# Four of eight experts' places shrink from 124 to 120 and one grows from 148 to 150 in an attention, mixture-of-experts and feed-forward kernel

## The chip, the core and the metric

The kernel runs on one core of a Trainium2 chip. The metric is device time in microseconds (us): the median of timed executions of the whole program. The profile beside it is of one execution of its own. TensorE is called PE below; its weight loads have a row of their own, PEld. VectorE is DVE, ScalarE is ACT, GpSimd is POOL, SyncE is SP. SP and ACT also issue transfers, which the core's 16 DMA engines carry out.

## What is computed

The reference has three stages over 2304 tokens. The middle one, which the change touches, sends each token that passes a skip test to one of eight experts:

```python
def _moe_ref(x, w_skip, w_gate, w1, w2):
    do_compute = (x @ w_skip) > 0
    xc = x[do_compute]
    logits = xc @ w_gate
    e_idx = np.argmax(logits, axis=1)
    gate_w = softmax(logits)[arange, e_idx]
    for e in range(8):
        mask = e_idx == e
        h = np.maximum(xc[mask] @ w1[e], 0.0)
        y[mask] = gate_w[mask, None] * (h @ w2[e])
    out[do_compute] = xc + y
```

Ahead of it stands masked attention (4 batches, 8 heads, 576 positions, 64 wide), whose output is `x`; behind it a feed-forward layer (512 to 2048 to 512) with a piecewise quadratic activation. For the reference's inputs the eight experts get 166, 153, 145, 136, 113, 111, 106 and 87 tokens, in order of size.

## The kernel before

**Stages.** Attention and the routing come first. At their end POOL scatters each token, as a row of 515 float32 (512 values, a gate weight, a token's number in two parts), to a scratch tensor `scr` in HBM, where each expert has a region of its own. Then the experts run one after the other, and after them the feed-forward layer, which fills the rest of the program.

**Places.** The experts are ranked by their number of tokens. An expert of rank r gets `RANKED[r]` columns in every tile of its stage, whatever its true number; `ORDER` has them run by rank as 0, 4, 1, 5, 2, 6, 3, 7, so `CAP` is 168, 124, 156, 124, 148, 124, 140, 124. An expert with more tokens than places would go on in a loop behind the stage (`tc.If(ovf > 1)`), in chunks of `CF` columns. `CF` is the smallest entry of `RANKED`; it also sets `NCHUNK`, the length of the tables that this loop would read.

**An expert's rows.** `load_x(e)` loads the expert's rows from `scr` in two halves of `CAP[e] // 2` rows each, as tiles `xr` with one row in each partition (L759). For expert 0 SP and ACT issue one half each, for all others SP issues both. `prep_x` turns a half into columns on PE: one transpose for the gate weight (L774), four for the values (L776), one for the number (L777).

**An expert's matmuls.** Eight steps f. `emit_h` multiplies a weight tile by the expert's columns (L818, four matmuls, each of which the trace records twice), ACT applies the rectifier (L820), and `emit_y`, two steps later, multiplies by a tile of the second weight (L838, again four). A weight tile `wr` is 128 by 1024 float32, 524,288 bytes; an expert has eight, of which `emit_h` uses the even ones, each for two steps, and `emit_y` the odd ones. So steps 0 and 1 need tile 0, steps 2 and 3 tile 2, and step 4 tile 4. The next expert's halves are turned behind steps 3 and 4.

**Order of the loads.** SP's queue is in program order: the halves of expert 0, four weight tiles, the halves of expert 1, four more weight tiles, a tile `sk` of skipped tokens, four more weight tiles, and so on. Tiles of weights share slots with the raw weights of the last layer, which DVE, ACT and POOL decode during the experts (`decode`). PE runs a few empty matmuls (`stay_warm`, L176) where it would else be idle.

Of the kernel before, what the change touches and what calls it, by code (L numbers as in the profile page):

```python
# [40 lines left out]
LK, SK = QT + STR, 5 * NJ  # L41


RANKED = (168, 156, 148, 140, 124, 124, 124, 124)
C, CF = RANKED[0], RANKED[-1]
ORDER = (0, 4, 1, 5, 2, 6, 3, 7)
CAP = [RANKED[r] for r in ORDER]
W = DM + 3
# [1078 lines left out]
```

## Time and profile before

| | before |
|---|---|
| median of 3 timed runs | 692.84 us (691.78 to 695.59) |
| the profiled execution's own time | 686.14 us |
| its span, first to last instruction | 684.5 us |
| PE busy | 657.0 us, 96% of the span |
| granted TensorE clock, mean | 0.994 |

The span is what the trace covers; the profiled execution's own time holds 1.64 us more around it. The timed runs are other executions: their median is 6.70 us above the profiled one.

### The profile page before, as it was taken

The numbers are of one execution on the slowest core, as the hardware profiler recorded it, in microseconds if no ns is written. First come the engines' busy times: TensorE is split into PE (matmuls) and PEld (weight loads), VectorE is DVE, ScalarE is ACT, GpSimd is POOL, SyncE is SP. The second block draws the span as 40 slices with busy tenths as digits, with TensorE's granted clock in tenths as the row PEclk, the third lists the DMA queues.
The fourth block names the chain that finished last, engine by engine and source line by source line (L and its number), as shares of the span: only waits on it lengthen the run. The fifth ranks groups of instructions, "written<-read, shape, count | busy, mean of one in ns | idle before, by whom it ended". The sixth has DMA issues, their size and how long they took to land.

```text
span 684.5 us, 13286 instructions
## 1 busy us (share of the span) xinstructions
PE 657.0 (96%) x4766; PEld 588.4 (86%) x4768; DVE 391.4 (57%) x1223; ACT 289.1 (42%) x783; POOL 110.0 (16%) x175
## 2 busy tenths in 40 slices
PE   8999997799999998999999999999999999999996
PEld 5787784699999988889998998999899989998994
DVE  6988976347676765777643354335544543454332
ACT  5776650233333332555533343334433433353332
POOL 6553644022222221000010001000100010001001
PEclk9999999899999999999999999999999999999999
DMA  9898993999789964021010001000100010001001
GB/s 267 237 283 252 331 351 142 340 332 312 242 276 300 335 234 166 32 88 36 1 47 0 1 1 46 1 1 0 47 1 0 1 47 0 1 1 46 1 1 46
DMA packets 24337, 82.95 MB, mean 121 GB/s; under 512 B 3446, under 2 KB 3446, under 8 KB 24266
## 3 DMA queue, kind: packets, MB, share of 16 engines
q1 hardware_dynamic: 19640, 68.28, 31.0%
q0 software_dynamic: 2880, 9.47, 3.7%
q10 hardware_dynamic: 1746, 4.30, 1.8%
q8 instruction: 39, 0.64, 0.4%
q14 instruction: 32, 0.26, 0.1%
HBM read 72.57 MB, written 9.46 MB: 120 GB/s over the span
## 4 chain that ended last, share of the span: by engine, by line
issue 46%; PE 10%; POOL 2%; DVE 0%; POOLq 0%; ACT 0%; ACTq 0%; DVEq 0%
PE hp L1009 6%; PE po L1046 5%; POOL out_dram L180 2%; POOLq L1123 0%; DVE x L1055 0%; ACT r L1019 0%; DVE r L1023 0%; DVE r L1024 0%; DVE gl L1032 0%; ACT gh L1028 0%; ACT xh L989 0%; POOLq L180 0%; PE hp L1013 0%; ACTq L989 0%; DVEq L1024 0%
## 5 line engine op out<-in xcount | busy, mean ns | idle before, releaser
L1009 PE MATMUL hp<-xh,wd 128*128 128x384 f32 x768 | 196.4, 337 | 2.4 <-ACT xh L989 2.4
L1046 PE MATMUL po<-wd,gh 128*128 128x512 f32 x576 | 180.5, 395 | 0.0
L1009 PEld LDWEIGHTS hp<-xh,wd 128*128 128x128 f32 x768 | 140.2, 188 | 10.8 <-ACT xh L989 2.6
L1023 DVE SCALAR_TENSOR_TENSOR r<-r 128x384 f32<-128x384 f32 x96 | 53.6, 558 | 134.8 <-ACT r L1019 134.7
L1009 PE MATMUL hp<-xl,wd 128*128 128x384 f32 x384 | 129.3, 337 | 0.0
L1046 PEld LDWEIGHTS po<-wd,gh 128*128 128x128 f32 x576 | 106.5, 188 | 17.1
L1046 PE MATMUL po<-wd,gl 128*128 128x512 f32 x288 | 113.4, 394 | 0.0
L1019 ACT ACTIVATE r<-hp,half 128x384 f32<-128x384 f32 x96 | 55.7, 580 | 136.4 <-PE hp L1009 122.9
L1028 ACT CAST gh<-r 128x384 fp32r<-128x384 f32 x96 | 49.3, 514 | 89.3 <-DVE r L1024 75.3
L1032 DVE TENSOR_TENSOR gl<-r,gh 128x384 fp32r<-128x384 f32 x96 | 53.6, 558 | 54.6 <-ACT gh L1028 54.4
L180 POOL DMA_INDIRECT out_dram<-x,outid x18 | 18.0, 998 | 396.4 <-DVE x L1055 336.2
L818 PE MATMUL hpt<-x,wr 128*128 128x124 f32 (+4 forms) x512 | 73.6, 287 | 3.8 <-DMA wr<-in_we_dram 3.8
L838 PE MATMUL yp<-h,wr 128*128 128x124 f32 (+4 forms) x512 | 74.5, 290 | 1.9 <-issue 1.9
L1009 PEld LDWEIGHTS hp<-xl,wd 128*128 128x128 f32 x384 | 72.1, 188 | 0.4 <-DVE xl L990 0.4
L818 PEld LDWEIGHTS hpt<-x,wr 128*128 128x128 f32 x512 | 67.4, 193 | 4.5 <-issue 4.5
L838 PEld LDWEIGHTS yp<-h,wr 128*128 128x128 f32 x512 | 66.8, 193 | 3.9 <-issue 2.6
L1046 PEld LDWEIGHTS po<-wd,gl 128*128 128x128 f32 x288 | 54.1, 188 | 12.5
L421 ACT ACTIVATE pe<-sm,nm 128x90 f32<-128x90 f32 (+1 forms) x144 | 52.1, 364 | 26.5 <-DVE nm L414 22.0
L1024 DVE TENSOR_TENSOR r<-r,hp 128x384 f32<-128x384 f32 x96 | 53.2, 554 | 10.9 <-DVE r L1023 0.9
L1021 ACT ACTIVATE hp<-hp,half 128x384 f32<-128x384 f32 x96 | 52.3, 545 | 0.0
L723 POOL TENSOR_TENSOR wd<-da,wd 128x512 fp32r<-128x512 f32 x25 | 32.4, 1298 | 117.9 <-ACT wd L708 91.9
L708 ACT CAST wd<-da 128x512 fp32r<-128x512 f32 x32 | 19.8, 619 | 49.7 <-DVE da L711 43.2
(167 smaller groups left out, 696.1 us busy)
## 6 DMA issues: line engine op xcount, KB each, us to landing
wr<-in_we_dram SPq DMA_DIRECT2D x64, 512.0 KB
qk<-in_qk_dram SPq DMA_DIRECT2D x16, 592.0 KB
raw<-in_w_in_dram SPq DMA_DIRECT2D x16, 512.0 KB
v<-in_v_dram SPq DMA_DIRECT2D x15, 432.0 KB
raw<-in_w_out_dram SPq DMA_DIRECT2D x9, 512.0 KB
raw<-in_w_out_dram ACTq DMA_DIRECT2D x7, 512.0 KB
sk<-scr SPq DMA_DIRECT2D x12, 257.5 KB
xr<-scr SPq DMA_DIRECT2D x8, 124.7 KB
```

Of the source, the lines that this page charges most:

```text
L421: nc.scalar.activation(r["pe"][:, t, :N], r["sm"][:, t, :N], AF.Exp, bias=r["nm"][:, t:t + 1], scale=-1.0, accum_out=r["su"][:, t:t + 1])
L723: lambda: (V if late else nc.gpsimd).tensor_tensor(s["lo"], s["a"], s["hi"].bitcast(F32), op=ALU.subtract),
L818: nc.tensor.matmul(hpt, w[:, o:o + P], xg[e][:, c, :], start=c == 0, stop=c == 3)
L838: nc.tensor.matmul(yps[e][m // 2][:, m % 2], w[:, o:o + P], h, start=f == 0 and m % 2 == 0, stop=f == 7 and m % 2 == 1)
L1009: nc.tensor.matmul(hpt, w[:, c * P:(c + 1) * P], x, start=k == 0, stop=k == 11)
L1019: nc.scalar.activation(r, hpt, AF.Relu, bias=half[:, 0:1], scale=0.5)
L1021: nc.scalar.activation(u, hpt, AF.Relu, bias=half[:, 1:2], scale=0.5)
L1023: nc.vector.scalar_tensor_tensor(g, r, 1.0, r, ALU.min, ALU.mult)
L1024: nc.vector.tensor_tensor(g, g, u, op=ALU.add)
L1028: nc.scalar.copy(gh, g)
L1032: nc.vector.tensor_tensor(gl, g, gh.bitcast(F32), op=ALU.subtract)
L1046: nc.tensor.matmul(ops[bi][m], a[:, c], b_, start=f == 0 and k == 0, stop=f == NF - 1 and k == 2)
```

## The change

One line: `RANKED`, the table of places. In the order in which they run the experts get 168, 120, 156, 120, 150, 120, 140, 120 columns instead of 168, 124, 156, 124, 148, 124, 140, 124; the halves of rows are 84, 60, 78, 60, 75, 60, 70, 60 instead of 84, 62, 78, 62, 74, 62, 70, 62. `CF` becomes 120, and with it `NCHUNK` 20 instead of 19. A blank line ahead of the table moves every line number behind it up by one.

```diff
+
-RANKED = (168, 156, 148, 140, 124, 124, 124, 124)
+RANKED = (168, 156, 150, 140, 120, 120, 120, 120)
 C, CF = RANKED[0], RANKED[-1]
 ORDER = (0, 4, 1, 5, 2, 6, 3, 7)
 CAP = [RANKED[r] for r in ORDER]
```

No instruction moves past another; shapes change where they stand. SP's queue at the head of the experts' stage, before, from the last two of the first four weight tiles to the first two of the next four (`xr` are the halves of expert 1, `wr` the weight tiles, the loads from `tab` and `etab` fetch their addresses):

```order
L211 DMA wr<-in_we_dram 128x1024
L211 ISA
L211 DMA wr<-in_we_dram 128x1024
L197 TENSOR_LOAD etab
L759 ISA
L759 DMA xr<-scr 62x515
L756 TENSOR_LOAD tab
L759 ISA
L759 DMA xr<-scr 62x515
L211 ISA
L211 DMA wr<-in_we_dram 128x1024
```

The same place of the change:

```order
L212 DMA wr<-in_we_dram 128x1024
L212 ISA
L212 DMA wr<-in_we_dram 128x1024
L198 TENSOR_LOAD etab
L760 ISA
L760 DMA xr<-scr 60x515
L757 TENSOR_LOAD tab
L760 ISA
L760 DMA xr<-scr 60x515
L212 ISA
L212 DMA wr<-in_we_dram 128x1024
```

The two loads have 60 rows instead of 62, and stand where they stood. PE in expert 0, before, from step 3 of the first product (L818) to step 4, with the first half of expert 1 turned between them and the second product of step 1 (L838) behind it:

```order
L818 MATMUL hpt<-x,wr 128x168 x4
L774 MATMUL xtp<-idt,xr 128x62
L776 MATMUL xtp<-idt,xr 128x62 x4
L777 MATMUL xtp<-idt,xr 2x62
L838 MATMUL yp_2618<-h,wr 128x168 x2
L838 MATMUL yp_2619<-h,wr 128x168 x2
L818 MATMUL hpt<-x,wr 128x168 x4
```

The same place of the change:

```order
L819 MATMUL hpt<-x,wr 128x168 x4
L775 MATMUL xtp<-idt,xr 128x60
L777 MATMUL xtp<-idt,xr 128x60 x4
L778 MATMUL xtp<-idt,xr 2x60
L839 MATMUL yp_2618<-h,wr 128x168 x2
L839 MATMUL yp_2619<-h,wr 128x168 x2
L819 MATMUL hpt<-x,wr 128x168 x4
```

The transposes are two columns narrower; the matmuls of expert 0 and their order are the same.

## Rows read from the trace of the kernel before

**Rows 1.** The page: the span

```profile
span 684.5 us, 13286 instructions
```

**Rows 2.** By stretch: busy us of PE, PEld, DVE, ACT, POOL; clock, DMA share, GB/s

```profile
128.70:134.40 5.70, 2.05 (x15) 1.54 (x14) 1.89 (x5) 1.61 (x4) 1.26 (x1) 0.90 1.04 327
134.40:140.20 5.80, 5.71 (x23) 5.17 (x24) 0.94 (x3) 1.29 (x3) 0.21 (x1) 0.51 1.03 404
148.00:268.00 120.00, 118.06 (x1013) 115.58 (x1012) 82.73 (x176) 43.12 (x111) 28.63 (x22) 1.00 0.83 281
268.00:684.50 416.50, 407.37 (x2070) 367.09 (x2069) 202.72 (x382) 171.17 (x335) 17.96 (x18) 1.00 0.05 19
```

**Rows 3.** Timeline of PE, 122 to 143 us: start, us, what; idle before, its end

```profile
122.67 3.88 PE L818 MATMUL hpt<-x,wr 128*128 128x168 f32 x24 [0.96 <-DMA wr<-in_we_dram]
...
127.54 1.30 PE L818 MATMUL hpt<-x,wr 128*128 128x168 f32 x8
129.69 0.27 PE L774 MATMUL xtp<-idt,xr 62*128 62x62 f32 x1 [0.85 <-DMA xr<-scr]
...
130.20 1.41 PE L838 MATMUL yp<-h,wr 128*128 128x168 f32 x8
134.49 2.58 PE L818 MATMUL hpt<-x,wr 128*128 128x168 f32 x8 [2.88 <-DMA wr<-in_we_dram]
136.99 0.36 PE L774 MATMUL xtp<-idt,xr 62*128 62x62 f32 x1
...
137.82 2.53 PE L838 MATMUL yp<-h,wr 128*128 128x168 f32 x8
140.19 1.30 PE L818 MATMUL hpt<-x,wr 128*128 128x168 f32 x8
141.33 1.30 PE L838 MATMUL yp<-h,wr 128*128 128x168 f32 x8
```

**Rows 4.** Timeline of SP's queue: issues at the head of the experts' stage

```profile
120.71 1.52 SPq L759 DMA_DIRECT2D xr<-scr  x2
...
129.67 0.33 SPq L211 DMA_DIRECT2D wr<-in_we_dram  x1
...
133.28 0.33 SPq L211 DMA_DIRECT2D wr<-in_we_dram  x1
```

**Rows 5.** Waits of SP's queue, 119 to 137 us: us, times, longest

```profile
SPq L211 <- DMA xr<-scr: 5.9, 2, 3.1
```

**Rows 6.** By stretch, columns as in rows 2: behind 62-row halves, with 78-row halves

```profile
144.00:147.00 3.00, 3.00 (x23) 2.98 (x22) 1.57 (x4) 1.10 (x3) 0.55 (x1) 1.00 1.04 233
...
178.60:180.80 2.20, 2.20 (x20) 2.17 (x19) 0.64 (x2) 1.33 (x3) 1.17 (x1) 1.00 0.16 54
```

**Rows 7.** Waits of SP's queue, 194 to 211 us (62-row halves): us, times, longest

```profile
SPq L211 <- DMA xr<-scr: 2.9, 1, 2.9
SPq L792 <- DMA xr<-scr: 2.4, 1, 2.4
```

**Rows 8.** Waits of PE, 148 to 268 us, all of them

```profile
PE yp L838 <- issue: 1.9, 2, 1.3
```

**Rows 9.** Timeline of PE: neighbouring groups of 124, 148 and 140 columns

```profile
188.89 1.05 PE L838 MATMUL yp<-h,wr 128*128 128x124 f32 x8
189.78 1.06 PE L818 MATMUL hpt<-x,wr 128*128 128x124 f32 x8
...
211.91 1.17 PE L818 MATMUL hpt<-x,wr 128*128 128x148 f32 x8
212.91 1.17 PE L838 MATMUL yp<-h,wr 128*128 128x148 f32 x8
...
248.88 1.12 PE L838 MATMUL yp<-h,wr 128*128 128x140 f32 x8
249.83 1.12 PE L818 MATMUL hpt<-x,wr 128*128 128x140 f32 x8
```

**Rows 10.** By stretch, columns as in rows 2: most of an expert with 124 columns

```profile
187.50:204.00 16.50, 16.50 (x152) 16.45 (x152) 13.00 (x28) 6.12 (x15) 3.83 (x3) 1.00 0.82 271
```

## The prediction

> **What bounds the kernel now.** I read the profile from the whole to the one place where this change can matter. The profiled execution took 686.14 us, of which the trace spans 684.5 [rows 1]. Next the stretches: in the feed-forward stage PE is busy for 407.37 of 416.50 us with the DMA engines at a share of 0.05, and from 148 to 268 us, over seven of the eight experts, PE is busy for 118.06 of 120.00 [rows 2]. There the length is set by what PE executes, and no load can shorten it. The list of PE's waits in that stretch agrees: 1.9 us in two waits, both ahead of L838 and neither for a transfer [rows 8].
>
> The exception is the head of the experts' stage. From 128.70 to 134.40 us PE is busy for 2.05 of 5.70 us, and in the next 5.80 us it is busy at a granted clock of 0.51 [rows 2], the lower of its two levels, 1.2 instead of 2.4 GHz. The timeline says what it stands for. It waits 0.85 us for `xr`, the first half of expert 1 (62 rows), then 2.88 us for a weight tile [rows 3]. By the program that is tile 4 of expert 0, the first one that SP issues behind the two halves of 62 rows. After this pause the same groups of 168 columns that later start 1.14 us apart (140.19 to 141.33) take 2.4 to 2.5 us: 134.49 to 136.99 and 137.82 to 140.19 [rows 3].
>
> Why is tile 4 late? The halves were issued at 120.71 us, and SP's two issues of weight tiles at 129.67 and 133.28 were held for 5.9 us in sum by `xr` loads [rows 4, 5]. So each half was in flight for over 9 us. They are small: 62 x 515 x 4 = 127,720 bytes each, against 524,288 in a weight tile. At the 404 GB/s of the stretch from 134.40 [rows 2] both together are 0.63 us of all 16 engines. What is special is how few engines carry them. Behind a later pair of 62-row halves, when most of the queue has drained, the DMA share falls to 0.16 at 54 GB/s while weights are still on their way [rows 6]; one engine's part of 404 GB/s is 25.25, so this is what two engines move, and 2 of 16 are a share of 0.125. 62 is 2 times 31, and has no larger divisor up to 16. Two engines are therefore busy with 127,720 bytes each for both halves, 127,720 / 25.25 GB/s = 5.06 us, while the other fourteen go on. Every weight tile is spread over all 16, so each tile behind the halves is complete only when the two late engines are through.
>
> The sum confirms it. Tile 0 ends a wait of PE at 122.67 [rows 3]. Tiles 1 to 4 are 4 x 524,288 / 404 GB/s = 5.19 us, and the halves on two engines 5.06: tile 4 at 132.92. The stretch from 128.70 moved 327 GB/s instead of 404 at the same share [rows 2], which is 5.7 x (1 - 327/404) = 1.09 us more, 134.01; PE got it at 134.49.
>
> **Part 1, the halves of 62 and 74 rows become 60 and 75.** 60 and 75 are 4 and 5 times 15, so by the same reading of the row they lie on 15 engines. Then both halves cost 0.63 us instead of 5.06, and tile 4 lands at 122.67 + 5.19 + 0.63 = 128.5. The upper bound: in the stretch 144 to 147, where halves of 78 rows go through, all engines together moved 233 instead of 404 GB/s [rows 6], a loss of 3.0 x (1 - 233/404) = 1.27 us; with it tile 4 lands at 129.8. When does PE want it? Without the first wait the transposes start at 129.69 - 0.85 = 128.84; they take 0.51 (129.69 to 130.20), and the group of L838 behind them 1.14 [rows 3]. So step 4 is ready at 130.5, 0.7 to 2.0 us behind the tile. The first half itself comes at about 122.67 + 3 x 1.30 + 0.32 = 126.9, ahead of 128.84. Both waits go. With no pause PE has no reason to lose its clock: before 128.70 it was fed without a break of more than 0.96 us [rows 3].
>
> What that is worth: 0.85 + 2.88 = 3.73 us of waiting, and the lower clock. From 134.49 to 140.19 are 5.70 us; the same three groups at full clock are 1.14 + 0.10 + 0.51 + 1.14 = 2.89, where 0.10 is an allowance for the change from wide matmuls to transposes. That gives 2.81, together 6.54 us. What is late next? Nothing that I see: two tiles at the low rate of 233 GB/s take 4.5 us, and PE uses two tiles in two steps, four groups of 1.14 = 4.6 us. Between 148 and 268 us the 62- and 74-row halves also hold SP (2.9 and 2.4 us in one example [rows 7]), but no wait of PE there is for a transfer [rows 8], so I put the faster loads there at nothing; the cover is PE's own work, and if it were gone there would be more to gain, not less.
>
> The Trainium skill (DMA: Bandwidth & Descriptors, section "Why a DMA increments its semaphore by 16 and not by 1") says the same as a rule: such a load runs on the largest number of engines up to 16 that divides its outer dimension. By it 62 and 74 rows use 2 engines, 60 and 75 use 15. The trace shows the two, and no row of it shows a load of 60 or 75 rows; by the rule the sum is the one above.
>
> **Part 2, columns of the matmuls.** A group (four matmuls, eight records) starts 0.95 us after its neighbour at 140 columns, 1.00 at 148, and 0.89 at 124 [rows 9]. From 140 to 148 one column is 0.00625 us a group. Expert 4 has 16 groups, so two columns more cost 16 x 2 x 0.00625 = 0.20 us. On the same line 124 columns would be 0.85, but the row says 0.89: there the columns no longer decide. PEld is busy for 16.45 of 16.50 us in such an expert [rows 10], so loading the weights sets the pace, and a load of 128 columns is the same for 120 places. I take nothing for 124 to 120. The other end, if the line held, is 4 experts x 16 groups x 4 columns x 0.00625 = 1.60 us gained; 0.89 above the line speaks for the first.
>
> The skill (TensorE: Matmul & The Clock Gate, section "LDWEIGHTS") has a rule against a gain here as well: a weight load takes its columns divided by 1.2, in ns, so 107 for 128 columns however few are streamed. The row gives 0.89 / 8 = 111. By the rule the sum is unchanged.
>
> **Part 3, the rest.** DVE, ACT and the transposes handle 2 to 4 columns less in four experts and 1 or 2 more in one; the cover is PE, busy throughout [rows 2]. The tables grow from 152 to 160 numbers on DVE, while the first loads are on their way; if that cover were gone it would be a few per cent of five short instructions.
>
> **Sum.** 6.54 - 0.20 = 6.3 us: span 678.2, the profiled execution's own time 679.8. The timed median lies 6.70 us above that of the profiled execution; I let this stand and take 692.84 - 6.3 = 686.5 us. 0.5% is 3.5 us, about what a measurement of this kernel can tell from no change.
>
> **The rivals.**
>
> *Tile 4 is late all the same.* For it: packets also slow down where 78-row halves are read [rows 6], and now all 15 engines write rows at once. If all bytes from 122.67 on (four tiles and two halves of 60 rows, 2.34 MB) moved at 233 GB/s, tile 4 would land at 132.7, 2.2 us behind 130.5. Then PE waits again, and may lose its clock again: the gain is 1.3 us with the loss of 2.81, 4.1 without, so 688.7 to 691.5. Against it: the slow stretch was 3 us, not 10.
>
> *The change doesn't spread the loads, or the timed runs don't have the pause.* No row shows 60 rows, and the timed runs have no trace. Then only part 2 is left: 693.0 us.
>
> *Slower: the loop behind the experts runs.* An expert of rank 4 or later with 121 tokens would go through `tc.If(ovf > 1)`, and another pass over its weights is about one expert of 124 columns, 16.5 us [rows 10]: 686.5 + 16.5 = 703. It decides at the 121st token; the largest of these experts has 113. Even a DMA rate of 233 GB/s throughout is no way to slower: 132.7 is still ahead of 134.49.
>
> **How the numbers follow.** Forecast 0.70: own range 683.0 (with the 1.60 us of the columns, and both waits of [rows 8] gone) to 687.8 (tile 4 on the edge, with decoding, which loses its rest, costing PE another wait of 1.3 us like the longer one of [rows 8]). Late tile 0.12, no effect 0.12, slower 0.06 (half of it the loop, half what I don't see). The range runs from the forecast's lower end to the end of the late tile: 683.0 to 691.5, which leaves out 0.18. Faster by over 0.5%: the forecast and a third of the late tile, 0.74; within: 0.20; slower: 0.06.
>
> **What would show it.** In the profile of the changed kernel: no wait of PE for `wr` between 124 and 145 us, and none for `xr` of expert 1; granted clock 1.00 throughout these stretches; groups 1.14 us apart from step 3 of expert 0 on; SP's waits for `xr` at the head of the stage well below 5.9 us; no stretch with a DMA share of 0.16 while weights are due. Groups of 120 columns 0.89 us apart, those of 150 columns 1.01 to 1.02. I am wrong if the wait of 2.88 us is still there with loads that land early (then it wasn't the halves), if it moves to a later tile, or if the timed runs gain nothing where the profiled one does.

## The result and the profile after

The changed kernel takes 687.15 us in the median of 8 runs (685.74 to 689.21), the kernel before 692.93 us (691.3 to 695.59) beside it. The ratio is 0.9916, with a 95% interval of 0.9895 to 0.9937: 5.8 us faster, between 4.4 and 7.3. The forecast was 686.5 us, from 683.0 to 691.5. (A ratio here and below is the one on record for runs beside each other; it can differ a little from the quotient of the two medians.)

The spans of the two profiled executions say something else at first sight: 684.0 us after, 684.5 before [rows 1], where the forecast had 678.2 after. They differ in four places, so they have to be taken apart by stage. Start of the first transposes of the experts' stage and start of the last matmul of its second product, first before, then after (one line of the program each: its records, their shortest, median and longest time in ns, first and last start):

```profile
L774 PE MATMUL xtp<-idt,xr x16: 226/261/363, 120.1 to 246.4; 62*128 62x62 f32 x8, 84*128 84x84 f32 x2, 78*128 78x78 f32 x2, 74*128 74x74 f32 x2
L838 PE MATMUL yp<-h,wr x512: 269/282/647, 126.4 to 270.6; 128*128 128x124 f32 x85, 128*128 128x168 f32 x22, 128*128 128x140 f32 x22, 128*128 128x156 f32 x21
```

```profile
L775 PE MATMUL xtp<-idt,xr x16: 226/260/263, 125.5 to 244.0; 60*128 60x60 f32 x8, 84*128 84x84 f32 x2, 78*128 78x78 f32 x2, 75*128 75x75 f32 x2
L839 PE MATMUL yp<-h,wr x512: 264/282/410, 131.2 to 267.3; 128*128 128x120 f32 x85, 128*128 128x168 f32 x22, 128*128 128x140 f32 x22, 128*128 128x156 f32 x21
```

The experts' stage, from the first to the last of these, went from 150.5 to 141.8 us, 8.7 less. Attention, which no shape of the change touches, ended 5.4 us later in this one execution. The turn from the experts to the feed-forward stage was 1.4 us longer (the clock fell to half for 3.4 us there), and the feed-forward stage itself 1.5 us longer. Attention and the turn vary from execution to execution: over the twelve kernels below the first transposes start between 120.1 and 128.6 us, and the execution of before that was shown has the earliest of all. That is probably where most of the 6.70 us between its own time and the timed median lay; the timed runs have no trace to show it. Of the change the profiled execution took 685.74 us, only 1.41 less than the timed median.

The head of the experts' stage after, PE's timeline, to be laid beside [rows 3]:

```profile
127.56 3.78 PE L819 MATMUL hpt<-x,wr 128*128 128x168 f32 x24 [0.42 <-DVE x L779]
...
132.32 1.30 PE L819 MATMUL hpt<-x,wr 128*128 128x168 f32 x8
133.56 0.26 PE L775 MATMUL xtp<-idt,xr 60*128 60x60 f32 x1
...
134.05 1.41 PE L839 MATMUL yp<-h,wr 128*128 128x168 f32 x8
135.30 1.30 PE L819 MATMUL hpt<-x,wr 128*128 128x168 f32 x8
136.53 0.26 PE L775 MATMUL xtp<-idt,xr 60*128 60x60 f32 x1
...
137.03 1.41 PE L839 MATMUL yp<-h,wr 128*128 128x168 f32 x8
138.27 1.30 PE L819 MATMUL hpt<-x,wr 128*128 128x168 f32 x8
139.41 1.30 PE L839 MATMUL yp<-h,wr 128*128 128x168 f32 x8
```

From the first step to step 4 (135.30) there are now 7.74 us, where there were 11.82, and no bracket: neither the transposes nor step 4 waits for a load. Step 5 follows 2.97 us behind step 4; it was 5.70 at the lower clock. The stretches after (columns as in [rows 2]) show the clock at 1.00, and a DMA rate of 340 GB/s up to 133.5 us and of 408 behind it:

```profile
127.50:133.50 6.00, 5.94 (x40) 5.72 (x40) 2.50 (x6) 1.55 (x5) 0.00 (x0) 1.00 1.02 340
133.50:139.30 5.80, 5.80 (x45) 5.34 (x45) 3.00 (x8) 2.90 (x7) 1.39 (x2) 1.00 1.03 408
148.00:268.00 120.00, 119.34 (x1030) 117.08 (x1029) 82.67 (x179) 43.15 (x110) 28.40 (x22) 1.00 0.84 288
268.00:684.00 416.00, 406.98 (x2039) 366.35 (x2036) 202.13 (x380) 171.11 (x334) 17.85 (x18) 0.99 0.05 18
```

SP's queue from 123 to 143 us after (wait, its end, us in total, times, longest) has no entry for `xr`, where [rows 5] had 5.9 us; its longest is this one:

```profile
SPq L212 <- DMA wr<-in_we_dram: 3.1, 4, 1.3
```

And PE's waits from 148 to 268 us, where [rows 8] had 1.9 us:

```profile
PE yp L839 <- issue: 0.7, 1, 0.7
```

### The profile page after: what moved, and what is told of

It is laid out like the page before. It is cut to its first block, busy times and chain, and to the rows that moved or that the text cites. A ratio compares the mean times of both kernels' runs of the same rounds, so it can differ in the third digit from the quotient of the medians.

```text
span 684.0 us, 13286 instructions
## 1 busy us (share of the span) xinstructions
PE 659.5 (96%) x4766; PEld 590.2 (86%) x4768; DVE 390.4 (57%) x1223; ACT 289.7 (42%) x783; POOL 109.6 (16%) x175
## 4 chain that ended last, share of the span: by engine, by line
issue 47%; PE 10%; POOL 2%; DVE 0%; POOLq 0%; ACT 0%; ACTq 0%; DVEq 0%
PE hp L1010 6%; PE po L1047 5%; POOL out_dram L181 2%; POOLq L1124 0%; DVE x L1056 0%; ACT r L1020 0%; DVE r L1024 0%; DVE r L1025 0%; DVE gl L1033 0%; ACT gh L1029 0%; ACT xh L990 0%; POOLq L181 0%; PE hp L1014 0%; ACTq L990 0%; DVEq L1025 0%
## 5 line engine op out<-in xcount | busy, mean ns | idle before, releaser
L1010 PEld LDWEIGHTS hp<-xh,wd 128*128 128x128 f32 x768 | 141.8, 189 | 10.8 <-ACT xh L990 2.5
L839 PE MATMUL yp<-h,wr 128*128 128x120 f32 (+4 forms) x512 | 73.4, 287 | 0.7 <-issue 0.7
L819 PE MATMUL hpt<-x,wr 128*128 128x120 f32 (+4 forms) x512 | 72.3, 285 | 0.4 <-DVE x L779 0.4
L435 POOL TENSOR_TENSOR pn<-pe,rc 128x288 f32<-128x288 f32 (+5 forms) x62 | 32.7, 548 | 41.5 <-DVE nm L415 22.3
(167 smaller groups left out, 684.5 us busy)
```

Source lines behind the costliest of these rows:

```text
L435: mul[e](r["pn"][:, t0:t1, :N], r["pe"][:, t0:t1, :N], r["rc"][:, t0:t1].unsqueeze(2).to_broadcast([P, t1 - t0, N]), op=ALU.mult)
L819: nc.tensor.matmul(hpt, w[:, o:o + P], xg[e][:, c, :], start=c == 0, stop=c == 3)
L839: nc.tensor.matmul(yps[e][m // 2][:, m % 2], w[:, o:o + P], h, start=f == 0 and m % 2 == 0, stop=f == 7 and m % 2 == 1)
L1010: nc.tensor.matmul(hpt, w[:, c * P:(c + 1) * P], x, start=k == 0, stop=k == 11)
```

## The experiments

For each kernel the stage was split in the same way, from the starts in its trace: the head from the first start of the transposes (L774) to the 29th record of the second product (L838), which is the middle of its group for step 3 of expert 0 and runs behind the first product of step 5; the rest of the experts' stage from there to the last start of L838; and the feed-forward stage by the first and last start of its second product (L1046). The line numbers are those of before; kernels made from the change have them one higher, e7_split three. The timed difference against before is in us (minus is faster), with its 95% interval, from the before that ran beside the kernel; e11_pad128 ran once. Each stage time is of one execution.

| kernel | head | rest | experts | L1046 | timed against before |
|---|---|---|---|---|---|
| before | 21.8 | 128.7 | 150.5 | 396.6 | |
| the change | 14.5 | 127.3 | 141.8 | 398.0 | -5.8 (-7.3 to -4.4) |
| e1_first | 17.0 | 127.6 | 144.5 | 396.6 | -7.1 (-9.1 to -5.0) |
| e2_rest | 20.4 | 127.3 | 147.8 | 398.0 | +1.7 (-0.3 to +3.7) |
| e3_61 | 24.9 | 127.5 | 152.5 | 396.6 | +3.6 (+1.6 to +5.5) |
| e4_64 | 15.2 | 130.1 | 145.3 | 396.6 | -4.1 (-6.1 to -2.0) |
| e6_warm | 18.8 | 130.9 | 149.8 | 396.6 | +0.3 (-1.3 to +2.1) |
| e7_split | 14.9 | 127.2 | 142.1 | 396.6 | -8.1 (-9.9 to -6.2) |
| e8_pad | 20.2 | 129.8 | 150.0 | 398.0 | +1.3 (-1.0 to +3.5) |
| e9_cf124 | 14.6 | 127.4 | 141.9 | 396.6 | -7.4 (-9.2 to -5.6) |
| e10_narrow | 14.8 | 127.2 | 142.0 | 396.6 | -8.5 (-10.1 to -6.8) |
| e11_pad128 | 21.2 | 129.4 | 150.6 | 397.3 | |

**Only the first of the small experts (e1_first).**

```diff
-RANKED = (168, 156, 148, 140, 124, 124, 124, 124)
+RANKED = (168, 156, 148, 140, 120, 124, 124, 124)
```

> Only the first of the four small experts to run gets 120 columns (halves of 60 rows); all other places stay as before. Theory (the first pair of 62-row halves, on two DMA engines, makes tile 4 of expert 0 late): the whole gain of the change, 5 to 7 us, 686 to 688 us; in the profile no wait of PE for a weight tile at step 4 of expert 0. Rival (the gain comes from fewer columns, or from all the lighter loads together): a quarter of it, 1 to 2 us, 691 to 692 us.

686.90 against 693.12 us, ratio 0.9898 (0.9868 to 0.9928). A quarter of the narrower places brings all of the gain that a timed run can see. The theory stands, the rival that counts columns doesn't. PE's timeline has step 4 right behind the group ahead of it, without a wait:

```profile
137.91 1.41 PE L838 MATMUL yp<-h,wr 128*128 128x168 f32 x8
139.16 1.30 PE L818 MATMUL hpt<-x,wr 128*128 128x168 f32 x8
```

The head in its profile is 17.0 us and not 14.5. The first groups of the stage ran at half clock there, from 126.7 us on, where a wait of 2.2 us for the very first rows ended, ahead of any load that was changed; in the profile of the change the clock stayed up behind such a wait of 2.17 us.

```profile
126.70:133.50 6.80, 6.61 (x34) 6.62 (x35) 1.12 (x5) 0.75 (x2) 0.00 (x0) 0.50 0.98 326
```

**The others, without the first (e2_rest).**

```diff
-RANKED = (168, 156, 148, 140, 124, 124, 124, 124)
+RANKED = (168, 156, 150, 140, 124, 120, 120, 120)
```

> The complement: the first small expert keeps 124 columns, the other three get 120 and the one of 148 gets 150. Theory: the wait for tile 4 is still there (2 to 4 us, with the lower clock behind it) and the time is that of before within 1 us, 692 to 694 us. Rival (columns, or all loads together): three quarters of the gain, 4 to 5 us, 688 to 689 us.

694.49 against 693.12 us, ratio 1.0024 (0.9995 to 1.0053): no gain. PE's timeline shows both waits and the lower clock as before:

```profile
135.15 0.27 PE L774 MATMUL xtp<-idt,xr 62*128 62x62 f32 x1 [0.73 <-DMA xr<-scr]
...
139.85 2.58 PE L818 MATMUL hpt<-x,wr 128*128 128x168 f32 x8 [2.79 <-DMA wr<-in_we_dram]
...
143.18 2.11 PE L838 MATMUL yp<-h,wr 128*128 128x168 f32 x8
145.13 1.30 PE L818 MATMUL hpt<-x,wr 128*128 128x168 f32 x8
```

The rest of the stage is 1.4 us shorter than before, though, which neither theory had. The lighter loads there are not shown to be the reason: e1_first and e3_61, which keep the 62-row halves of the later experts, have nearly the same rest (127.6 and 127.5 us).

**61 rows (e3_61).**

```diff
-RANKED = (168, 156, 148, 140, 124, 124, 124, 124)
+RANKED = (168, 156, 148, 140, 122, 124, 124, 124)
```

> The first small expert gets 122 columns, fewer than before: halves of 61 rows, a prime number, all else as before. Theory: one DMA engine carries both halves, 2 x 61 x 2060 bytes at 25.25 GB/s = 10.0 us instead of 5.06, so tile 4 comes about 5 us later still and the kernel is slower than before by 4 to 7 us, 697 to 700 us. Rival (fewer columns or fewer bytes help): 0 to 1 us faster than before.

697.41 against 693.12 us, ratio 1.0052 (1.0023 to 1.0080): two columns fewer, and slower. Both waits have grown, and at 0.50 the clock stays low for the next 5.8 us (timeline, then the stretch):

```profile
136.19 0.26 PE L774 MATMUL xtp<-idt,xr 61*128 61x61 f32 x1 [2.06 <-DMA xr<-scr]
...
143.60 2.58 PE L818 MATMUL hpt<-x,wr 128*128 128x168 f32 x8 [5.51 <-DMA wr<-in_we_dram]
```

```profile
143.60:149.40 5.80, 5.80 (x23) 5.23 (x24) 0.94 (x3) 1.29 (x3) 0.30 (x1) 0.50 0.94 330
```

The two waits are 7.6 us, 3.8 more than before; expected were 5 more. The mean of the interval is 3.6 us, a little under the 4 that were the lower end. The direction, on which the rival differs, is clear.

The trace also shows how many engines such a load has. While little but the first half of 61 rows is under way, the DMA engines move 26 GB/s, one engine's part of 404 being 25.25; behind 62 rows it was 54 [rows 6]:

```profile
131.20:132.00 0.80, 0.80 (x8) 0.80 (x7) 0.35 (x1) 0.53 (x2) 0.00 (x0) 1.00 0.07 26
```

The packets of single rows (2,060 bytes each) say the same. From the first of them on, until other rows join them, exactly one is under way for 8.9 us here, and exactly two for 5.8 us before. In the change all 120 rows pass in 2.05 us, with up to 13 under way at once; in e4_64 (below) it is 128 rows in 2.99 us with up to 14, and in e7_split (below) 124 rows in 2.29 us with up to 15.

**64 rows (e4_64).**

```diff
-RANKED = (168, 156, 148, 140, 124, 124, 124, 124)
+RANKED = (168, 156, 148, 140, 128, 124, 124, 124)
```

> The first small expert gets 128 columns, more than before: halves of 64 rows, four for each of 16 engines; all else as before. Theory: the wait goes as with 60 rows, and 16 groups of 128 columns cost at most 16 x 4 x 0.00625 = 0.4 us: 5 to 7 us faster than before, 686 to 688 us. Rival (columns): 0 to 1.5 us slower than before, 693 to 694.5 us.

690.12 against 693.12 us, ratio 0.9941 (0.9912 to 0.9971). More columns than before and faster: the rival is out. But the gain, 4.1 us, is under the 5 to 7 expected. The head has its full gain (15.2 us). What is lost is in the rest, where PE's waits from 136 to 268 us are these:

```profile
PE xtp L774 <- DMA xr<-scr: 1.4, 2, 0.8
PE yp L838 <- issue: 1.4, 2, 0.9
```

The two halves that PE waits for are one of 74 rows and one of 62 (195.4 and 213.7 us), still slow to load. Why they are late here is not settled: e1_first, which has the same later halves, has no wait for `xr` there. Its PE came later by 1.8 us in the head, which may be what hid them.

**Empty matmuls over the pause (e6_warm).** In the loop over the steps:

```diff
+                if i == 4:
+                    stay_warm(40)
                 emit_h(e, f)
```

> The kernel before, with 40 empty matmuls ahead of step 4 of expert 0, about 3 us of work for PE while tile 4 is on its way; the loads are as before. Theory (2.9 us of the gain are waiting, 2.8 us the lower clock that follows): tile 4 is as late as before, but the groups behind it are 1.14 us apart, and the kernel is 2 to 3 us faster than before, 690 to 691 us. Rival (the clock falls for another reason, or its loss is made up later): same as before within 1 us.

690.73 against 689.83 us, ratio 1.0005 (0.9981 to 1.0030): no gain. The edit did what it should: the empty matmuls fill the pause, step 4 follows at once (12.00 us behind the first step, 11.82 before), and the groups behind are at full clock:

```profile
136.01 3.13 PE L176 MATMUL hpt<-warm 128*128 128x168 bf16 x40
139.10 1.38 PE L818 MATMUL hpt<-x,wr 128*128 128x168 f32 x8
...
142.16 1.30 PE L818 MATMUL hpt<-x,wr 128*128 128x168 f32 x8
143.30 1.30 PE L838 MATMUL yp<-h,wr 128*128 128x168 f32 x8
```

The head is 1.4 to 3.0 us shorter than in the three kernels with the loads and the head of before (20.2 to 21.8). Most of that is given back in the rest, 130.9 us (128.7 to 129.8 in those three), where PE waits from 140 to 268 us for

```profile
PE xtp L774 <- DMA xr<-scr: 2.0, 2, 1.3
PE yp L838 <- issue: 1.8, 2, 1.0
```

So the theory falls in its second half: the lower clock is real, but curing it alone is worth nothing that can be measured. In this profile the halves of 74 and 62 rows further on were next in line; e8_pad, with the same loads, also waits 1.0 us for one of them.

**The same places, loads split (e7_split).**

```diff
-                    eng.dma_start(r, scr[ds(row + NT, n), :])
+                    k = 60 if n == 62 else n
+                    eng.dma_start(r[:k], scr[ds(row + NT, k), :])
+                    if k < n:
+                        eng.dma_start(r[k:n], scr[ds(row + (NT + k), n - k), :])
```

> The places of before, with each half of 62 rows loaded as two transfers of 60 and 2 rows: the same columns and bytes, eight transfers more in SP's queue. Theory (only the number of engines matters): the wait for tile 4 goes, 5 to 7 us faster than before, 686 to 688 us. Rival (columns, or the number of transfers in the queue): no gain, or slower by the extra issues, 693 to 696 us.

682.63 against 689.83 us, ratio 0.9883 (0.9856 to 0.9910). No place is changed, no byte saved and eight transfers added, and the gain is no smaller than that of the change. Step 4 has no wait:

```profile
134.10 1.41 PE L841 MATMUL yp<-h,wr 128*128 128x168 f32 x8
135.35 1.30 PE L821 MATMUL hpt<-x,wr 128*128 128x168 f32 x8
```

With the packets shown under e3_61, that leaves the number of engines that a half lies on as the cause.

**A longer table (e8_pad).** `fbt` and its two writes:

```diff
-    fbt = keep.tile([1, 2, NE * NCHUNK], I32, name="fbt")
+    fbt = keep.tile([1, 2, NE * (NCHUNK + 1)], I32, name="fbt")
```

> The kernel before, with the table for the loop behind the experts 64 bytes longer, as the change makes it, and nothing else. In the profiles with the longer table (the change and the complement) the feed-forward stage from its 61st matmul on takes 387.57 us, in the others 386.11. Theory (what lies behind the table in SBUF is shifted, and that costs TensorE 1.46 us there): 387.6 us. Rival (the chunk size or something else of the change): 386.1 us. The timed median is that of before plus 1 to 2 us or plus 0, which this measurement hardly tells apart; the verdict is by the profile.

The feed-forward stage's second product, in before, in this kernel and in the change:

```profile
L1046 PE MATMUL po<-wd,gh x576: 387/394/498, 280.8 to 677.1; 128*128 128x512 f32 x192
```

```profile
L1046 PE MATMUL po<-wd,gh x576: 387/392/501, 283.5 to 681.3; 128*128 128x512 f32 x192
```

```profile
L1047 PE MATMUL po<-wd,gh x576: 387/392/501, 278.9 to 676.7; 128*128 128x512 f32 x192
```

396.3, 397.8 and 397.8 us by this one form (the table's figures, 0.2 to 0.3 us longer, take in a second form of it). From the 61st matmul of the first product to the last of the second the trace has 386.11 us in before and 387.57 here, to the hundredth as in the change. The 64 bytes alone cost 1.46 us by the trace. The timed ratio, 1.0019 (0.9986 to 1.0051), doesn't tell that from nothing.

**The change with the table of before (e9_cf124).**

```diff
 RANKED = (168, 156, 150, 140, 120, 120, 120, 120)
-C, CF = RANKED[0], RANKED[-1]
+C, CF = RANKED[0], 124
```

> The change, with the chunk size kept at 124, so that the table is as long as before. Theory: the head of the experts' stage as in the change (no wait for tile 4), and the feed-forward stage at 386.1 us instead of 387.6: 1.5 us faster than the change, 6 to 8 us faster than before, 685 to 687 us. Rival (the 1.46 us come from the places): 387.6 us there, and the time of the change.

681.98 against 689.83 us, ratio 0.9893 (0.9866 to 0.9919). The experts' stage is that of the change (141.9 us), and the feed-forward stage that of before:

```profile
L1047 PE MATMUL po<-wd,gh x576: 387/394/499, 276.2 to 672.5; 128*128 128x512 f32 x192
```

396.3 us. That stage is 1.5 us shorter than in the change; the timed intervals of the two overlap.

**Narrower still (e10_narrow).** On top of e9_cf124:

```diff
-RANKED = (168, 156, 150, 140, 120, 120, 120, 120)
+RANKED = (168, 156, 150, 140, 120, 112, 112, 96)
```

> The change with the chunk size of 124, and the last three small experts at 112, 112 and 96 columns instead of 120 (halves of 56, 56 and 48 rows, on 14, 14 and 16 DMA engines); they hold 111, 106 and 87 tokens. From the first transpose of the experts' stage to its last matmul the change with the chunk size of 124 took 141.7 us. Theory (below some 130 columns the weight loads set TensorE's pace, 0.89 us a group): 141.2 to 142.2 us, groups of 112 and 96 columns 0.89 us apart, and the time of that kernel. Rival (0.00625 us for each column of a group): 16 x (8 + 8 + 24) x 0.00625 = 4.0 us less, 137.7 us, and 4 us faster.

685.07 against 693.66 us, ratio 0.9878 (0.9854 to 0.9902). The stage takes 142.0 us, 0.1 more than in e9_cf124, and groups of 112 and of 96 columns start 0.89 and 0.90 us apart:

```profile
195.03 1.06 PE L839 MATMUL yp<-h,wr 128*128 128x112 f32 x8
195.92 1.06 PE L819 MATMUL hpt<-x,wr 128*128 128x112 f32 x8
...
257.58 1.06 PE L839 MATMUL yp<-h,wr 128*128 128x96 f32 x8
258.48 1.06 PE L819 MATMUL hpt<-x,wr 128*128 128x96 f32 x8
```

The rival's 4.0 us aren't there.

**A table longer by 128 bytes (e11_pad128).** As e8_pad, with `NCHUNK + 2`; one execution, of 696.85 us.

> The kernel before with the table for the loop behind the experts 128 bytes longer instead of 64. Theory (any shift of what lies behind the table costs): the second product of the feed-forward stage runs over 397.8 us from its first to its last matmul, as with 64 bytes. Rival (it depends on where in a block of 128 bytes the data lie): 396.3 us, as in the kernel before.

```profile
L1046 PE MATMUL po<-wd,gh x576: 387/394/496, 290.7 to 687.8; 128*128 128x512 f32 x192
```

397.1 us, between the two answers: neither theory. Its head has the waits of before.

## Why the prediction was right, point by point

**The late tile.** Right, and shown from five sides. 62 rows: two waits and a fallen clock in before, e2_rest, e8_pad and e11_pad128, while in e6_warm empty matmuls fill the pause; 60 rows, 64 rows, or 60 + 2: no wait there; 61 rows: longer waits than 62, with less data. The rule of the Trainium skill (DMA: Bandwidth & Descriptors, section "Why a DMA increments its semaphore by 16 and not by 1"), by which 61 rows run on one engine, 62 on two, 60 on 15 and 64 on 16, agrees with all of them; for 61 and 62 rows the trace shows the number itself (under e3_61), for 60 and 64 only that it is many. The first half was in flight for 8.98 us at most (120.71 to 129.69), not over 9. The step was put at 6.54 us. Between the two profiles shown the head lost 7.3 us. Over the kernels with the head of before (before, e2_rest, e8_pad, e11_pad128) it is 20.2 to 21.8, mean 20.9; with 60, 64 or 60 + 2 rows (the change, e4_64, e7_split, e9_cf124, e10_narrow; e1_first left out for its half clock at the start) 14.5 to 15.2, mean 14.8: 6.1 us.

**When PE wants tile 4.** The forecast margin of 0.7 to 2.0 us was enough: SP's queue and PE's timeline show no wait. The DMA engines ran at 340 GB/s up to 133.5 us, so the slowing that the rival feared was there in part, and at 408 behind it, the full rate of [rows 2]. The rival of a tile that is late all the same is out.

**"I put the faster loads there at nothing."** Right for the trace that it was read from, where none of PE's waits in the rest was for a load [rows 8], and open beyond it. The slack there was small. e8_pad, with the same loads, has a wait of 1.0 us for `xr`; in e4_64 and e6_warm, where 64 rows or empty matmuls cured the head alone, such waits add up to 1.4 and 2.0 us, and the rest is 130.1 and 130.9 us. Where the 62-row halves are gone from the rest too it is 127.2 to 127.4, in five kernels of five. But e1_first and e3_61 keep them and have 127.6 and 127.5. So in these profiles the lighter loads are worth anything from next to nothing to 3.7 us; what they are worth in the timed runs is not shown. A part of the difference is waits of L838 whose releaser the trace doesn't name: 1.9 us before, 0.7 after, and 0.7 in e1_first and e3_61 as well. What takes them away is open.

**The lower clock.** Its row was read rightly: step 5 now follows 2.97 us behind step 4, where the sum had 2.89. As a term by itself the 2.81 us are not confirmed: with the clock kept up and the loads of before (e6_warm) the experts' stage is only 0.2 to 0.8 us shorter than in the three kernels with the same loads, and the timed runs show nothing. In e1_first the waits and the pause in front of step 4 go together, and the whole gain comes, though the later halves stay as they were.

**The columns.** Right: 120 columns are 0.89 us a group like 124, and so, within 0.01, are 112 and 96. That the weight loads set this floor is argued, from PEld's being busy for 16.45 of 16.50 us [rows 10]; the runs show the floor. Groups of 150 columns start 1.02 us apart, 0.02 over 148, where the sum had 0.0125. Both from the timeline after:

```profile
195.49 1.05 PE L839 MATMUL yp<-h,wr 128*128 128x120 f32 x8
196.38 1.06 PE L819 MATMUL hpt<-x,wr 128*128 128x120 f32 x8
...
210.07 1.19 PE L819 MATMUL hpt<-x,wr 128*128 128x150 f32 x8
211.09 1.18 PE L839 MATMUL yp<-h,wr 128*128 128x150 f32 x8
```

**The rest of the edits.** Wrong in one of them. The longer table was priced by the instructions that fill it. It cost 1.46 us in a stage some 150 us later, which doesn't read it; that it does so by where it puts the data behind it is argued, no view shows a place. In the two profiles the gain in the rest of the experts' stage (1.4 us) nearly cancels it. That the sum of 6.3 came out so close is luck in that part.

**The sum.** By the profiles it is 8.7 - 1.5 = 7.2 us, the timed runs say 5.8 with 7.3 as the end of the interval. For the other kernels the same sum of stages lies inside the timed interval, but for e2_rest: 2.7 - 1.5 = 1.2 us faster by the stages, 0.3 faster to 3.7 slower by the timed runs. One profile each doesn't settle that. That the gain carries over to the timed runs was assumed, and it held. The forecast of 679.8 us for the profiled execution itself did not: it took 685.74, above all because attention ended 5.4 us later in it than in the one of before.

## What to carry to other kernels

Look at how a small load divides over the DMA engines before asking how many bytes it has: here 2 x 62 rows held back the weight tile behind them, for which PE waited 2.88 us, and two rows fewer, two rows more, or the same rows in two transfers all cured it. When such a load is cured at one place, look at its copies further on, whose waits may only have been hidden by the first. And a longer buffer can cost something where nothing reads it: compare a stage that the edit doesn't touch, to the hundredth, between two traces.

## What was not expected of the hardware

A table in SBUF longer by 64 bytes made the feed-forward stage 1.46 us longer (387.57 us in all three kernels with such a table, 386.11 in all eight with the table of before), and one longer by 128 bytes 0.72 us, in one execution. The extra time is spread over some 2,000 matmuls: between two neighbours the distance grows by 15 ns at most, and no wait holds it. Which access is slower is open. Attention and the routing took between 120.1 and 128.6 us in twelve profiles; in before the clock was at 1.00 from 7 to 120 us, in the others at half for one to three short periods; in the profile after PE got single matmuls some 0.75 us apart from 81 to 83 us, with no releaser in the trace. Its cause wasn't looked for.
